# Remainder matmuls of a first MLP product run two at a time in halves of the array, at the head of groups of four column blocks

## The chip, the cores and the metric

One core of one Trainium2 chip. The metric is the device time of one execution in microseconds; the median of several executions is given, and the profile is that of one execution. "Ratio" always means the mean time of one kernel's fast runs over the mean of the other's fast runs in the same rounds on the same chip, so it is not quite the ratio of the medians that stand beside it. Brackets after a ratio are its 95% interval.

## The reference

Two layers, each an attention block and an MLP block, over 2048 tokens of width D = 576:

```python
x = x + attention(layernorm(x))      # 32 heads of 18, causal window of 256, softmax
y = layernorm(x)                     # no scale, no bias
h = gelu(y @ w1 + b1)                # w1: 576 x 4608
x = x + h @ w2 + b2                  # w2: 4608 x 576
```

What matters here is 576 = 4 x 128 + 64. A matmul contracts over at most 128 rows, so `y @ w1` takes four full steps and a remainder of 64 rows.

## The kernel before

The kernel is a list of tasks for five engines. A planner in the Python code places the tasks in time by estimated costs, chooses PSUM banks (the accumulators in which matmul results are collected, eight here), and so fixes the order of the instructions of each engine; the engines then run that order, each waiting on semaphores. A changed cost constant therefore changes nothing but the order.

Tokens go through in 8 chunks of 512 columns (four of each layer). In a chunk, `G_part` makes one half of the first MLP product: 18 column blocks of 128, each accumulated in one bank over five matmuls of 512 columns, and a gelu on ScalarE. `mm2` then makes the second product, with 288-column matmuls. Attention scores (`scores`) are matmuls with 32 rows; four of them run side by side in four strips of the array. [...] marks cuts.

```python
    B_O = 7                # bank of the attention output
    FILL = (6, 5, 4)       # banks of mm2, QKV, output projection
    MM1 = (0, 1, 2, 3)     # banks of the first MLP product
    SC = (0, 2, 4)         # bank pairs of the scores

    def mm_cost(n):        # the planner's cost of a matmul of n columns, us
        return max(n / 2400.0, 0.026) + (0.006 if n > 64 else 0.0)

    [...]  # start: rows 64 to 127 of the fifth chunk of w1, wqkv, wo and the columns 576 to 639 of xn are set to zero once
        add("dve", lambda e: e.memset(w1_sb[64:128, :, 2048:2560], 0.0), writes=["w1Z"], cost=1.0, prio=-8)

    [...]  # G_part: a tile w1_sb[:, sl] holds four column blocks
        for f in range(hf * NFH, (hf + 1) * NFH):
            sl = (k * 9 + f // 4) % NB1
            fl = f - hf * NFH
            bk = Bank(MM1)

            def fn(e, f=f, sl=sl, bk=bk):
                ins = None
                for c in range(KD):
                    col = c * 512 + (f % 4) * 128
                    ins = e.matmul(bank(bk)[:, 0:n], w1_sb[:, sl, col:col + 128], xnTm[:, k % 2, c, 0:n], start=(c == 0), stop=(c == KD - 1))
                return ins
            add("pe", fn, reads=[f"w1a{sl}", f"w1b{sl}_0", "w1Z"] + TXm, writes=[bk], cost=mm_cost(n) * 5, prio=prio, lat=0.15, alloc=[bk], fifo="pa",
                after=[f"h{fl}"])
            add("act", lambda e, f=f, fl=fl, bk=bk: e.activation(hT[:, fl, 0:n], bank(bk)[:, 0:n], ACT.Gelu_apprx_tanh,
                                                                bias=b1col[:, f:f + 1]),
                reads=[bk, "b1"], writes=[f"h{fl}"], cost=0.2 + n * 0.00087, lat=0.2, fifo="act", prio=prio)
            if f % 4 == 3:
                w1_load(prio - 2)

    [...]  # scores: four 32-row strips
                for j in range(4):
                    ins = e.matmul(two(bs[j // 2])[:, j % 2, col:col + nq * 128], kT[32 * j:32 * j + 32, g, (T0 + so) % KS, :],
                                   qT[32 * j:32 * j + 32, g, qo * 128:(qo + nq) * 128], start=True, stop=True, tile_position=(32 * j, 0))
```

The fifth matmul of a block (`c = 4`) has 64 rows of data and 64 rows of zeros. It costs as much as a full one: all 90 matmuls of a half stage step by the same 216 ns (next section).

The softmax here doesn't subtract the row's maximum and nothing guards it: scores larger than these inputs give would overflow.

## Time and profile before

| | before |
|---|---|
| median of 3 runs (lowest to highest) | 987.5 us (986.23 to 987.52) |
| span of the profiled execution | 987.9 us |
| PE, ScalarE, VectorE, GpSimd busy | 96%, 59%, 32%, 37% |
| first MLP product begins | 120.1 us |

PE is the matrix engine and PEld its weight loads; ACT is ScalarE, DVE VectorE, POOL GpSimd, SP the engine that issues most DMAs. The span is the time from the first instruction of the profiled execution to the last.

The page first: its part 1 (busy time and share of the span, by engine) and part 4 (the chain of work that ended last, by engine and by line). Line 751 is the first MLP product, 776 the second, 558 and 564 QKV and output projection, 628 the scores, 675 the attention output.

```profile
PE 949.5 (96%) x9592; PEld 606.9 (61%) x9592; DVE 317.1 (32%) x772; ACT 586.0 (59%) x705; POOL 368.8 (37%) x507
...
PE 78%; DMA 5%; DVE 5%; POOL 5%; ACT 4%; issue 3%; DVEq 0%; POOLq 0%
PE ps L776 29%; PE ps L751 27%; PE ps L558 7%; PE ps L675 7%; PE ps L628 6%; ACT pT L637 3%; POOL pT L658 2%; DMA attT<-attq 2%; DVE x_res L709 2%; PE ps L564 2%; POOL rstd L499 2%; DVE st_all L486 2%; DMA x_res<-in_A_x_dram 1%; DMA kT<-qn 
```

Three quarters of the chain is PE. PE is what the kernel waits for, and the first MLP product is 27% of the span.

Then groups of instructions of before, one line for each shape: line, engine, operation, output and inputs, shapes, count; busy time and mean duration of one; idle time of the engine before them and what ended it.

```profile
L751 PE MATMUL ps<-xnTm,w_sb 128*128 128x512 bf16 x1440 | 319.4, 379 | 0.1
L776 PE MATMUL ps<-w_sb,hT 128*128 128x288 bf16 x2304 | 316.1, 288 | 6.0 <-DVE x_res L709 4.9 <-DVE xn L712 1.1
...
L755 ACT ACTIVATE hT<-ps,b1col 128x512 bf16<-128x512 f32 x288 | 196.5, 687 | 251.1 <-PE ps L751 250.8
...
L628 PE MATMUL ps<-qT,kT 32*128 32x256 bf16 x448 | 24.3, 280 | 6.7 <-ACT pT L637 6.5
```

PE sat idle 0.1 us in all before the 1440 matmuls of the first product: they are on the critical path. The mean duration, 379 ns, is no cost, because matmuls overlap in the pipeline. The cost is the step from one start to the next, and it is read from the timeline of PE (start, duration of the merged row, line, count). One half stage of before:

```profile
910.32 19.59 PE L751 MATMUL ps<-xnTm,w_sb 128*128 128x512 bf16 x90
929.75 3.47 PE L776 MATMUL ps<-w_sb,hT 128*128 128x288 bf16 x27
```

Ninety matmuls from 910.32 to 929.75 us are 216 ns each, so a block costs five times that, 1.08 us. The same view in a stretch with scores:

```profile
384.65 1.63 PE L776 MATMUL ps<-w_sb,hT 128*128 128x288 bf16 x12
386.22 0.40 PE L628 MATMUL ps<-qT,kT 32*128 32x256 bf16 x8
386.55 0.91 PE L776 MATMUL ps<-w_sb,hT 128*128 128x288 bf16 x6
```

Twelve matmuls of 288 columns step by 122 ns, so the last starts at 384.65 + 11 x 0.122 = 385.99 us, and the first score follows 0.23 us later, not 0.122. Over the whole trace the median of that step is 218 ns, and it is 312 ns behind a 512-column matmul: 96 ns more than without a change of mode, either time. (The mode is the way the array is divided: whole, in halves or in strips.) On the way out, the step is 200 ns behind scores of 256 columns, where the next set of scores otherwise follows after 110, and 264 behind 384 columns, where it follows after 163. Behind 128 columns it is 147; the 53 ns at which the prediction puts these columns are an estimate (94 ns for the 224 columns between 288 and 512 give 54 for 128). So the way out costs some 90 to 101 ns more than the columns.

The waits of PE in before (who waited for whom: us in total, times, longest) are few and short:

```profile
PE ps L628 <- ACT pT L637: 8.4, 18, 1.4
PE ps L558 <- DVE qn L594: 5.0, 5, 1.0
PE ps L776 <- DVE x_res L709: 4.9, 10, 0.6
...
PE ps L675 <- ACT hT L755: 0.5, 3, 0.2
```

### The profile page before, as it was taken

What the parts mean: (1) busy time and instruction counts of PE and PEld (TensorE: products, weight loads), DVE (VectorE), ACT (ScalarE), POOL (GpSimd) and SP (SyncE); (2) the same over time, 40 slices, a digit from 0 to 9 for tenths busy, and PEclk for the clock granted to TensorE, in tenths of its full rate; (3) what the DMA queues carried; (4) which work ended last, traced back from release to release, by engine and by line L of the source; (5) the groups of instructions that cost most, each with busy time, mean ns of one, the idle gap of its engine ahead of it and who ended that gap; (6) DMA issues with size and microseconds to landing.
All of it is one profiled execution on the core that took longest, in us unless ns stands there. A gap on an engine that the chain in (4) does not pass through costs nothing.

```text
span 987.9 us, 22924 instructions
## 1 busy us (share of the span) xinstructions
PE 949.5 (96%) x9592; PEld 606.9 (61%) x9592; DVE 317.1 (32%) x772; ACT 586.0 (59%) x705; POOL 368.8 (37%) x507
## 2 busy tenths in 40 slices
PE   8898889999999999999999999999999999999998
PEld 6665547655575656756476565756567564657556
DVE  5653612722145211534028130361115310132001
ACT  0476676377753777447761777627774487852531
POOL 4555725334333434325153252433333352531000
PEclk9999899999999999999999999999999999999999
DMA  9846380964269250881529542494516816084540
GB/s 195 173 116 136 74 253 15 208 174 138 68 145 192 60 178 28 188 187 34 191 56 204 136 126 80 133 170 106 169 49 167 177 44 198 14 220 118 172 132 25
DMA packets 227287, 129.58 MB, mean 131 GB/s; under 512 B 141808, under 2 KB 225008, under 8 KB 227184
## 3 DMA queue, kind: packets, MB, share of 16 engines
q1 hardware_dynamic: 217872, 120.43, 49.4%
q0 software_dynamic: 6880, 5.03, 2.7%
q10 hardware_dynamic: 2432, 2.65, 0.9%
q8 instruction: 76, 1.25, 0.5%
q14 instruction: 27, 0.22, 0.1%
HBM read 90.69 MB, written 2.36 MB: 94 GB/s over the span
## 4 chain that ended last, share of the span: by engine, by line
PE 78%; DMA 5%; DVE 5%; POOL 5%; ACT 4%; issue 3%; DVEq 0%; POOLq 0%
PE ps L776 29%; PE ps L751 27%; PE ps L558 7%; PE ps L675 7%; PE ps L628 6%; ACT pT L637 3%; POOL pT L658 2%; DMA attT<-attq 2%; DVE x_res L709 2%; PE ps L564 2%; POOL rstd L499 2%; DVE st_all L486 2%; DMA x_res<-in_A_x_dram 1%; DMA kT<-qn 1%; DVE xn L509 1%
## 5 line engine op out<-in xcount | busy, mean ns | idle before, releaser
L637 ACT ACTIVATE pT<-ps 128x1024 bf16<-128x1024 f32 (+2 forms) x384 | 347.2, 971 | 128.1 <-PE ps L628 126.9
L658 POOL TENSOR_SCALAR_AFFINE_SELECT pT<-pT 128x512 bf16<-128x512 bf16 (+1 forms) x368 | 278.1, 778 | 388.2 <-ACT pT L637 365.4
L755 ACT ACTIVATE hT<-ps,b1col 128x512 bf16<-128x512 f32 x288 | 196.5, 687 | 251.1 <-PE ps L751 250.8
L776 PE MATMUL ps<-w_sb,hT 128*128 128x288 bf16 x2304 | 316.1, 288 | 6.0 <-DVE x_res L709 4.9
L751 PE MATMUL ps<-xnTm,w_sb 128*128 128x512 bf16 x1440 | 319.4, 379 | 0.1
L776 PEld LDWEIGHTS ps<-w_sb,hT 128*128 128x128 bf16 x2304 | 211.2, 98 | 80.6 <-issue 20.2
L751 PEld LDWEIGHTS ps<-xnTm,w_sb 128*128 128x128 bf16 x1440 | 139.5, 98 | 159.6 <-issue 0.4
L709 DVE TENSOR_TENSOR x_res<-ps,x_res 128x288 f32<-128x288 f32 x160 | 70.7, 449 | 363.4 <-PE ps L776 342.6
L558 PE MATMUL ps<-wqkv,xnTa 128*128 128x288 bf16 x768 | 120.5, 286 | 8.9 <-DVE qn L594 5.0
L675 PEld LDWEIGHTS ps<-vA,pT 128*128 128x128 bf16 x2880 | 94.2, 96 | 29.2 <-issue 11.7
L675 PE MATMUL ps<-vA,pT 128*128 128x20 bf16 x2880 | 100.6, 172 | 5.6 <-DVE attq L690 2.7
L558 PEld LDWEIGHTS ps<-wqkv,xnTa 128*128 128x128 bf16 x768 | 71.2, 97 | 33.1 <-DVE qn L594 7.8
L628 PE MATMUL ps<-qT,kT 32*128 32x384 bf16 (+2 forms) x1408 | 75.0, 280 | 11.6 <-ACT pT L637 8.4
L594 DVE CAST qn<-ps 128x288 bf16<-128x288 f32 x128 | 57.4, 455 | 39.2 <-PE ps L564 38.3
L486 DVE BATCH_NORM_STATS2 st_all<-x_res 128x6 f32<-128x288 f32 x120 | 50.8, 446 | 17.2 <-DMA x_res<-in_A_x_dram 15.9
L509 DVE TENSOR_SCALAR xn<-x_res,mv_all,rstd 128x576 bf16<-128x576 f32 x60 | 47.2, 801 | 26.1 <-POOL rstd L499 14.6
L564 PE MATMUL ps<-wqkv,xnTa 128*128 128x288 bf16 x192 | 54.9, 286 | 0.0
L628 PEld LDWEIGHTS ps<-qT,kT 32*128 32x128 bf16 x1408 | 22.4, 92 | 49.0 <-issue 24.7
L733 POOL TENSOR_TENSOR x_res<-x_res,b2bc 128x576 f32<-128x576 f32 x32 | 45.2, 1415 | 13.7 <-DVE xn L509 12.9
L712 DVE TENSOR_TENSOR xn<-ps,x_res 128x288 bf16<-128x288 f32 x32 | 14.6, 458 | 110.9 <-PE ps L776 110.9
L497 POOL TENSOR_SCALAR vtmp<-mv_all 128x1 f32<-128x1 f32 (+1 forms) x43 | 8.6, 200 | 103.9 <-DVE mv_all L488 101.4
L685 DVE RECIPROCAL rinv<-ps 128x16 f32<-128x16 f32 x64 | 16.4, 257 | 95.7 <-PE ps L675 95.4
(32 smaller groups left out, 332.7 us busy)
## 6 DMA issues: line engine op xcount, KB each, us to landing
w_sb<-in_B_w_dram SPq DMA_DIRECT2D x144, 288.0 KB, 5.1
w_sb<-in_B_w_dram SPq DMA_DIRECT2D x72, 512.0 KB, 4.0
w_sb<-in_B_w_dram SPq DMA_DIRECT2D x72, 64.0 KB, 3.7
x_res<-in_A_x_dram POOLq DMA_DIRECT2D x4, 1152.0 KB, 7.0
out_dram<-xn SPq DMA_DIRECT2D x16, 144.0 KB, 1.8
wqkv<-in_A_wqkv_dram ACTq DMA_DIRECT2D x3, 576.0 KB, 5.9
hT<-in_A_x_dram SPq DMA_DIRECT2D x1, 576.0 KB, 5.2
wo_sb<-in_A_wo_dram ACTq DMA_DIRECT2D x1, 576.0 KB, 4.0
```

Of the source, the lines that this page charges most:

```text
L486: add("dve", lambda e, i=i, s=s: e.bn_stats(st_all[:, t, i, :], s[:, t, i * HB:(i + 1) * HB]), reads=res, writes=[f"st{t}_{i}"], cost=0.43 ...
L558: ins = e.matmul(bank(bs[o])[:, 0:n], lhs(o, c, full), rhs(o, c, full), start=(c == 0), stop=False)
L564: ins = e.matmul(bank(bs[o])[:, 0:n], lhs(o, 4, full), rhs(o, 4, full), start=False, stop=True)
L594: add("dve", lambda e, o=o, b=bs[o], qv=qv: e.tensor_copy(qv[:, o * 16:(o + 1) * 16, 0:DH], bank(b)[:, 0:HB].rearrange("p (h d) -> p h d", ...
L628: ins = e.matmul(two(bs[j // 2])[:, j % 2, col:col + nq * 128], kT[32 * j:32 * j + 32, g, (T0 + so) % KS, :], qT[32 * j:32 * j + 32, g, qo ...
L637: add("act", lambda e, h2=h2: e.activation(pT[:, sl, 2 * h2:2 * h2 + 2, lo:hi], two(bs[h2])[:, :, lo:hi], ACT.Exp, scale=SCALE), reads=[bs ...
L658: add("pool", lambda e, ap=ap, pat=pat, sgn=sgn, kind=kind: e.affine_select(ap, ap, pattern=pat, compare_op=(ALU.is_ge if kind == "d" else ...
L675: ins = e.matmul(bank(B_O)[:, o:o + VW], pT[:, sl, j, col + qi * 128:col + (qi + 1) * 128], vA[:, (T0 + so) % VS, 4 * g + j, :], start=(fi ...
L709: add("dve", lambda e: e.tensor_tensor(x_res[:, t, sl], bank(b)[:, 0:HB], x_res[:, t, sl], ALU.add), reads=[b], writes=[f"x{t}h{hh}"], cos ...
L751: ins = e.matmul(bank(bk)[:, 0:n], w1_sb[:, sl, col:col + 128], xnTm[:, k % 2, c, 0:n], start=(c == 0), stop=(c == KD - 1))
L755: add("act", lambda e, f=f, fl=fl, bk=bk: e.activation(hT[:, fl, 0:n], bank(bk)[:, 0:n], ACT.Gelu_apprx_tanh, bias=b1col[:, f:f + 1]), rea ...
L776: ins = e.matmul(bank(b)[:, 0:HB], hT[:, fl, i * 128:(i + 1) * 128], w2_sb[:, fl, hh * HB:(hh + 1) * HB], start=(fl == 0), stop=(fl == NFH ...
```

## The change

The intent is to run two 64-row remainders at once, one in the lower and one in the upper half of the array, into two banks. Because changing between full and half mode costs time, the remainders of four blocks are run together at the head of a group, which needs four banks at once, and so the product may use all seven banks. The 18 blocks of a half stage give groups of 4, 4, 4, 4, 2 or 2, 4, 4, 4, 4. To feed the upper half, the remainder of w1 is loaded in two parts, and an extra VectorE instruction writes the last 64 normalised columns a second time. The planner's constant goes from 0.006 to 0.003 us. The rest of the diff removes an unused option (`PAIR`). Cut to its core:

```diff
-    MM1 = (0, 1, 2, 3)
+    MM1 = (0, 1, 2, 3, 4, 5, 6)
-        return max(n / 2400.0, 0.026) + (0.006 if n > 64 else 0.0)
+        return max(n / 2400.0, 0.026) + (0.003 if n > 64 else 0.0)
[...]
-            dma("sp", w1_sb[0:64, sl, 2048:2560], B_w1[512:576, cols], reads=["w1Z"], writes=[f"w1b{sl}_0"], ...)
+        src = B_w1[512:576, cols].rearrange("p (a b f) -> p b a f", a=2, b=2)
+        for b in range(2):
+            dma("sp", w1_sb[64 * b:64 * b + 64, sl, 2048:2304].rearrange("p (a f) -> p a f", a=2), src[:, b], ...)
[...]
-        for f in range(hf * NFH, (hf + 1) * NFH):          # one block: five full matmuls
+        while f < f1:
+            n4 = min(4 - f % 4, f1 - f)
+            fs = range(f, f + n4)
+            bks = [Bank(MM1) for _ in fs]
+            def rest(e, fs=fs, sl=sl, bks=bks):
+                for ff, bk in zip(fs, bks):
+                    b = ff % 2
+                    col = 2048 + (ff % 4) // 2 * 128
+                    ins = e.matmul(bank(bk)[:, 0:n], w1_sb[64 * b:64 * b + 64, sl, col:col + 128], xnTm[64 * b:64 * b + 64, k % 2, 4, 0:n],
+                                   start=True, stop=False, tile_position=(64 * b, 0))
+            add("pe", rest, reads=rd, writes=bks, cost=mm_cost(n) * (n4 // 2) + 0.21, alloc=bks, fifo="pa", ...)
+            for ff, bk in zip(fs, bks):                     # then four full matmuls a block, and its gelu
+                [...]
```

More of the change, by code (lines that the diff above doesn't have):

```diff
@@ L331, in schedule @@
         return max(t.end for t in self.tasks)
-PAIR = False
-W1W = 2560
 WARM_UNTIL = 140.0
@@ L373, in build_kernel @@
     x_res = sb("x_res", [P, NT, D], FP32)
-    w1_sb = sb("w1_sb", [P, NB1, W1W], BF16)
+    w1_sb = sb("w1_sb", [P, NB1, 2304], BF16)
     w2_sb = sb("w2_sb", [P, NFH, D], BF16)
@@ L449, in build_kernel @@
     add("pool", lambda e: e.memset(nhalf[:, :], -0.5), writes=["nhalf"], cost=0.1, prio=-10)
-    if not PAIR:
-        add("pool", lambda e: e.memset(xn[:, :, D:KD * 128], 0.0), writes=[f"xn{i}" for i in range(NXN)], cost=0.4, prio=-10)
+    add("pool", lambda e: e.memset(xn[:, :, D:KD * 128], 0.0), writes=[f"xn{i}" for i in range(NXN)], cost=0.4, prio=-10)
     add("pool", lambda e: e.memset(vA[:, :, :, DH:VW], 1.0), writes=[f"v{s}h{h}" for s in range(VS) for h in range(2)], cost=1.6, prio=-8)
@@ L455, in build_kernel @@
             writes=[f"qn{i}h{h}" for h in range(2)], cost=0.5, prio=-9)
-    if not PAIR:
-        add("pool", lambda e: e.memset(attq[:, :, D:KD * 128], 0.0), writes=["aqd"], cost=0.5, prio=-8)
-        add("dve", lambda e: e.memset(wqkv[64:128, 4, :], 0.0), writes=["wqC", "wkC", "wvC"], cost=1.0, prio=-8)
-        add("dve", lambda e: e.memset(wo_sb[64:128, 4, :], 0.0), writes=["woC"], cost=0.4, prio=-8)
-        add("dve", lambda e: e.memset(w1_sb[64:128, :, 2048:2560], 0.0), writes=["w1Z"], cost=1.0, prio=-8)
+    add("pool", lambda e: e.memset(attq[:, :, D:KD * 128], 0.0), writes=["aqd"], cost=0.5, prio=-8)
+    add("dve", lambda e: e.memset(wqkv[64:128, 4, :], 0.0), writes=["wqC", "wkC", "wvC"], cost=1.0, prio=-8)
+    add("dve", lambda e: e.memset(wo_sb[64:128, 4, :], 0.0), writes=["woC"], cost=0.4, prio=-8)
     dma("pool", b2bc[:, :], bass.AP(tensor=B_b2.tensor, offset=B_b2.offset, ap=[[0, P], [1, D]]), writes=["b2"], cls="b", ring=2,
@@ L502, in build_kernel, with ln_norm_T @@
     xn_ctr = [0]
-    def ln_norm_T(t, i, dst, dname, prio, src=None, srcres=None):
+    def ln_norm_T(t, i, dst, dname, prio, src=None, srcres=None, dup=False):
         s = x_res if src is None else src
@@ L512, in ln_norm_T @@
         rd = [f"xn{sl}"]
-        if PAIR:
+        if dup:
             add("dve", lambda e: e.tensor_scalar(xn[:, sl, D:KD * 128], s[:, t, 512:D], mv_all[:, t, 0:1], rstd[:, t:t + 1],
@@ L533, in w1_load @@
             reads=reads, writes=[f"w1a{sl}"], cls="w1", cost=0.5, prio=prio)
-        if PAIR:
-            src = B_w1[512:576, cols].rearrange("p (a b f) -> p b a f", a=2, b=2)
-            for b in range(2):
-                dma("sp", w1_sb[64 * b:64 * b + 64, sl, 2048:2304].rearrange("p (a f) -> p a f", a=2), src[:, b],
-                    writes=[f"w1b{sl}_{b}"], cls="w1", cost=0.5, prio=prio)
-        else:
-            dma("sp", w1_sb[0:64, sl, 2048:2560], B_w1[512:576, cols], reads=["w1Z"], writes=[f"w1b{sl}_0"], cls="w1", cost=0.5,
-                prio=prio)
+        src = B_w1[512:576, cols].rearrange("p (a b f) -> p b a f", a=2, b=2)
+        for b in range(2):
+            dma("sp", w1_sb[64 * b:64 * b + 64, sl, 2048:2304].rearrange("p (a f) -> p a f", a=2), src[:, b],
+                writes=[f"w1b{sl}_{b}"], cls="w1", cost=0.5, prio=prio)
     def w2_load(hf, prio, gate=False):
@@ L547, in w2_load, with two_out @@
                 reads=[f"h{2 * pr}"] if gate else [], writes=[f"w2s{pr}"], cls="w2", ring=9, cost=0.6, prio=prio)
-    def two_out(lhs, rhs, n, reads, prio, after=()):
+    def two_out(lhs, rhs, reads, prio, after=()):
         bs = [Bank(FILL), Bank(FILL)]
-        full = slice(0, 128)
         for o in range(2):
@@ L556, in fn @@
                 ins = None
-                for c in range(4):
-                    ins = e.matmul(bank(bs[o])[:, 0:n], lhs(o, c, full), rhs(o, c, full), start=(c == 0), stop=False)
-                if PAIR and o == 1:
-                    for oo in range(2):
-                        r = slice(64 * oo, 64 * oo + 64)
-                        ins = e.matmul(bank(bs[oo])[:, 0:n], lhs(oo, 4, r), rhs(oo, 4, r), start=False, stop=True, tile_position=(64 * oo, 0))
-                if not PAIR:
-                    ins = e.matmul(bank(bs[o])[:, 0:n], lhs(o, 4, full), rhs(o, 4, full), start=False, stop=True)
-                return ins
-            w = [bs[0], bs[1]] if (o == 1 and PAIR) else [bs[o]]
-            cost = mm_cost(n) * (4 if PAIR else 5) + (mm_cost(n) * 1.2 if PAIR and o == 1 else 0.0)
-            add("pe", fn, reads=reads, writes=w, cost=cost, prio=prio, alloc=((bs if o == 0 else ()) if PAIR else [bs[o]]), after=after)
+                for c in range(KD):
+                    ins = e.matmul(bank(bs[o])[:, 0:HB], lhs(c), rhs(c, o * HB), start=(c == 0), stop=(c == KD - 1))
+                return ins
+            add("pe", fn, reads=reads, writes=[bs[o]], cost=mm_cost(HB) * KD, prio=prio, alloc=[bs[o]], after=after)
         return bs
@@ L579, in qkv @@
             dest = [f"v{A % VS}h{o}" for o in range(2)] if w == "v" else [f"qn{qn_ctr[0] % NQN}h{o}" for o in range(2)]
-            bs = two_out(lambda o, c, r: xnTa[r, c, i * 128:(i + 1) * 128],
-                         lambda o, c, r, n=n: wqkv[r, c, n * D + o * HB:n * D + (o + 1) * HB], HB,
+            bs = two_out(lambda c: xnTa[:, c, i * 128:(i + 1) * 128], lambda c, s, n=n: wqkv[:, c, n * D + s:n * D + s + HB],
                          [f"w{w}A", f"w{w}B", f"w{w}C", f"xa{i}"], prio + 0.01 * n, after=dest)
@@ L717, in tail @@
         rd = [f"aq{g}" for g in range(G)]
-        if PAIR:
-            add("dve", lambda e: e.tensor_copy(attq[:, 0:nt, D:KD * 128], attq[:, 0:nt, 512:D]), reads=rd, writes=["aqd"], cost=0.25,
-                prio=prio)
         for i in range(nt):
@@ L725, in tail @@
             t = t0 + i
-            bs = two_out(lambda o, c, r, i=i: attT[r, c, i * 128:(i + 1) * 128],
-                         lambda o, c, r: wo_sb[r, c, o * HB:(o + 1) * HB], HB, [f"aT{i}", "woA", "woB", "woC"], prio)
+            bs = two_out(lambda c, i=i: attT[:, c, i * 128:(i + 1) * 128], lambda c, s: wo_sb[:, c, s:s + HB],
+                         [f"aT{i}", "woA", "woB", "woC"], prio)
             for o in range(2):
@@ L731, in tail @@
             ln_rstd([t], True, prio)
-            ln_norm_T(t, i, xnTm[:, k % 2], f"xm{k % 2}_", prio)
+            ln_norm_T(t, i, xnTm[:, k % 2], f"xm{k % 2}_", prio, dup=True)
             add("pool", lambda e, t=t: e.tensor_tensor(x_res[:, t, :], x_res[:, t, :], b2bc[:, :], ALU.add),
@@ L741, in G_part @@
         TXm = [f"xm{k % 2}_{i}" for i in range(nt)]
-        for f in range(hf * NFH, (hf + 1) * NFH):
-            sl = (k * 9 + f // 4) % NB1
-            fl = f - hf * NFH
-            bk = Bank(MM1)
-            def fn(e, f=f, sl=sl, bk=bk):
-                ins = None
-                for c in range(KD):
-                    col = c * 512 + (f % 4) * 128
-                    ins = e.matmul(bank(bk)[:, 0:n], w1_sb[:, sl, col:col + 128], xnTm[:, k % 2, c, 0:n], start=(c == 0), stop=(c == KD - 1))
-                return ins
-            add("pe", fn, reads=[f"w1a{sl}", f"w1b{sl}_0", "w1Z"] + TXm, writes=[bk], cost=mm_cost(n) * 5, prio=prio, lat=0.15, alloc=[bk], fifo="pa",
-                after=[f"h{fl}"])
-            add("act", lambda e, f=f, fl=fl, bk=bk: e.activation(hT[:, fl, 0:n], bank(bk)[:, 0:n], ACT.Gelu_apprx_tanh,
-                                                                bias=b1col[:, f:f + 1]),
-                reads=[bk, "b1"], writes=[f"h{fl}"], cost=0.2 + n * 0.00087, lat=0.2, fifo="act", prio=prio)
-            if f % 4 == 3:
+        f1 = (hf + 1) * NFH
@@ new lines, in G_part, with fn @@
+        f = hf * NFH
+        while f < f1:
+            n4 = min(4 - f % 4, f1 - f)
+            fs = range(f, f + n4)
+            f += n4
+            sl = (k * 9 + fs[0] // 4) % NB1
+            bks = [Bank(MM1) for _ in fs]
+            rd = [f"w1a{sl}", f"w1b{sl}_0", f"w1b{sl}_1"] + TXm
+            def rest(e, fs=fs, sl=sl, bks=bks):
+                ins = None
+                for ff, bk in zip(fs, bks):
[3 more added lines that the diff above has]
+                                   start=True, stop=False, tile_position=(64 * b, 0))
+                return ins
+            add("pe", rest, reads=rd, writes=bks, cost=mm_cost(n) * (n4 // 2) + 0.21, prio=prio, alloc=bks, fifo="pa",
+                after=[f"h{ff - hf * NFH}" for ff in fs])
+            for ff, bk in zip(fs, bks):
+                fl = ff - hf * NFH
+                def fn(e, ff=ff, sl=sl, bk=bk):
+                    ins = None
+                    for c in range(4):
+                        col = c * 512 + (ff % 4) * 128
+                        ins = e.matmul(bank(bk)[:, 0:n], w1_sb[:, sl, col:col + 128], xnTm[:, k % 2, c, 0:n], start=False, stop=(c == 3))
+                    return ins
+                add("pe", fn, reads=rd, writes=[bk], cost=mm_cost(n) * 4, prio=prio, lat=0.15, fifo="pa")
+                add("act", lambda e, ff=ff, fl=fl, bk=bk: e.activation(hT[:, fl, 0:n], bank(bk)[:, 0:n], ACT.Gelu_apprx_tanh,
+                                                                      bias=b1col[:, ff:ff + 1]),
+                    reads=[bk, "b1"], writes=[f"h{fl}"], cost=0.2 + n * 0.00087, lat=0.2, fifo="act", prio=prio)
+            if fs[-1] % 4 == 3:
```

## The prediction

> **What bounds the kernel now.** TensorE. The page gives PE 96% busy; the chain of waits puts 78% of the span on PE (29% second MLP matmul, 27% first). Busy time overstates pipelined matmuls, so I count start to start: in PE's timeline a 512-column matmul of the first MLP product takes 216 ns, a 288-column one 122, a 20-column one 25. Such steps sum to about 793 of the 848 us after 140 us; about 30 us of the rest is switching to and from the 32-row score matmuls, some 25 us waits. The other engines have slack (ScalarE 59%).
>
> **What the change does.** Today each of 288 column blocks runs 5 matmuls of 512 columns, the fifth half zeros. Afterwards 4 full ones; the 64-row remainders run as 144 pairs, in 80 groups (64 of four blocks, 16 of two, because 18 blocks per half don't divide by four).
> - Removed: 288 x 0.216 = 62.2 us.
> - Added: 144 pairs. The Trainium skill (TensorE: Matmul & The Clock Gate, Part 3) says matmuls in different row groups run together, about 4 ns apart; the trace agrees: scores in four 32-row strips start 3 ns apart, and the next set follows 163 ns after 384 columns. So 0.219 us a pair: 31.5 us.
> - Added: 80 mode switches in and out. The skill (TensorEngine Tiling, Key Properties) says changing mode drains the array, without a figure. The trace shows it at the scores: from a full 512-column matmul to the first score 312 ns instead of 216 (96 extra); out of the scores 147 where 128 columns need 53 (94 extra). So 0.19 us a group: 15.2 us, an estimate carried over from 32-row to 64-row strips.
>
> Net on PE: 62.2 - 31.5 - 15.2 = 15.5 us. A group of two gains only 0.02.
>
> **Critical path.** Nearly all first-MLP matmuls lie on it: PE waits 0.1 us before them (groups).
>
> Given back: a group needs four banks at once, keeps the later ones about 3 us longer, and takes banks that the second MLP matmul, QKV and scores use too. Over 16 half stages I allow 1 to 3 us of new waits, where a group, or the first scores after it, waits for gelus. The extra VectorE copy of 64 columns and 72 more DMA issues on the SP queue are off the path. The finer cost constant reorders the plan; either sign, a few us.
>
> **Prediction: 973.5 us (-1.4%), 8 in 10 within 966 to 982. Faster by over 2%: 0.13; within 2%: 0.84; slower by over 2%: 0.03.**
>
> **What would show each step right or wrong.**
> - Groups: 1152 full 512-column matmuls and 288 with 64 rows; in the timeline the two of a pair start 3 ns apart, pairs 216 ns apart. If they serialise, the time rises by up to 31 us.
> - The step from a full matmul into a remainder about 312 ns, and out of it about 310. If switching costs 0.4 us a group, the gain is gone; if nothing, it is about 30 us.
> - Waits: PE on ScalarE before remainders or scores, under 5 us more than now.
> - A closed group of four takes about 4.1 us of PE, against 4.32.
>
> **What would make it wrong.** A 64-row switch that costs differently; a second pair whose weights cannot load behind the first; bank starvation where second-MLP matmuls and groups share seven banks; a plan that runs PE dry where exponentials limit.

## The result, and the profile after

| | before | after |
|---|---|---|
| median of 6 runs | 987.51 us (986.23 to 989.44) | 972.62 us (969.24 to 973.67) |
| ratio | | 0.9841 [0.982, 0.9861] |
| span of the profiled execution | 987.9 us | 967.4 us |
| PE busy | 96% | 96% |

The profiled execution of the changed kernel was the fastest of its six (969.24 us), so its trace shows 20.5 us of difference where the medians show 14.9. In later calls the same kernel gave 0.9822 and 0.9806. It is about 15 to 20 us faster, some 1.8%.

The same two parts of the page after. Line 748 is now the full matmuls of the first product, 736 its remainders, 772 the second product, 548 QKV and output projection, 609 the scores, 656 the attention output.

```profile
PE 933.4 (96%) x9596; PEld 582.3 (60%) x9596; DVE 324.6 (34%) x803; ACT 588.0 (61%) x705; POOL 370.5 (38%) x507
...
PE 82%; DMA 6%; POOL 4%; DVE 3%; issue 2%; ACT 2%; SPq 0%; POOLq 0%; DVEq 0%
PE ps L772 29%; PE ps L748 24%; PE ps L548 12%; PE ps L656 7%; PE ps L609 6%; PE ps L736 4%; POOL pT L639 2%; ACT pT L618 2%; DMA attT<-attq 2%; DVE x_res L690 1%; DMA xnTa<-xn 1%; DVE st_all L481 1%; DMA x_res<-in_A_x_dram 1%; DMA kT<-qn 1
```

The groups of the changed kernel; 509 is the added VectorE copy:

```profile
L772 PE MATMUL ps<-w_sb,hT 128*128 128x288 bf16 x2304 | 316.8, 288 | 5.6 <-DVE x_res L690 3.6 <-ACT hT L751 1.0 <-DVE xn L693 0.8
...
L748 PE MATMUL ps<-xnTm,w_sb 128*128 128x512 bf16 x1152 | 266.3, 380 | 0.0
...
L751 ACT ACTIVATE hT<-ps,b1col 128x512 bf16<-128x512 f32 x288 | 197.9, 688 | 215.7 <-PE ps L748 215.1
...
L736 PE MATMUL ps<-xnTm,w_sb 64*128 64x512 bf16 x288 | 45.0, 382 | 0.9 <-ACT pT L618 0.9
...
L509 DVE TENSOR_SCALAR xn<-x_res,mv_all,rstd 128x64 bf16<-128x64 f32 x32 | 10.9, 340 | 0.0
```

There are 1152 full matmuls and 288 with 64 rows, as intended. Gelu takes what it took (197.9 against 196.5 us).

A half stage of the changed kernel in the timeline of PE, to be held against the 90 matmuls in one row before:

```profile
927.81 0.39 PE L736 MATMUL ps<-xnTm,w_sb 64*128 64x512 bf16 x2
928.13 1.90 PE L748 MATMUL ps<-xnTm,w_sb 128*128 128x512 bf16 x8
929.96 0.61 PE L736 MATMUL ps<-xnTm,w_sb 64*128 64x512 bf16 x4
930.50 3.63 PE L748 MATMUL ps<-xnTm,w_sb 128*128 128x512 bf16 x16
934.06 0.60 PE L736 MATMUL ps<-xnTm,w_sb 64*128 64x512 bf16 x4
934.60 3.63 PE L748 MATMUL ps<-xnTm,w_sb 128*128 128x512 bf16 x16
```

From one head to the next, 929.96 to 934.06, a group of four takes 4.10 us; before it took 20 x 0.216 = 4.32. A group of two (927.81 to 929.96) takes 2.15 us against 2.16 before. The four remainders and the switch out take 0.54 us (929.96 to 930.50); the switch in lies in the step before. Inside, the two of a pair start 3 to 4 ns apart, and the second pair follows 222 to 224 ns after the first in 62 of the 64 groups of four. The median step from a full 512-column matmul into a remainder is 312 ns, and from a remainder to a full one 308.5.

The waits of PE after, none of which grew to anything:

```profile
PE ps L609 <- ACT pT L618: 4.3, 10, 1.3
PE ps L656 <- POOL pT L639: 3.8, 7, 1.4
PE ps L772 <- DVE x_res L690: 3.6, 6, 1.2
...
PE ps L736 <- ACT pT L618: 0.9, 2, 0.7
```

The first MLP product waited for banks 0.9 us in all.

I summed the steps between the starts of successive matmuls, from the first matmul of the first MLP product to the end, in the trace of each kernel. A step's nominal part is its columns' time (216 ns for 512 columns, 122 for 288, 25 for 20). A switch of mode is counted as 0.095 us each way, so the switches of the table are a count of switches times that price, and no measured sum. What lies above is a wait, or, in stretches where the records give half the TensorE clock, clock loss. In some traces 3 to 5% of the records of the full matmuls are missing; their time was put back from the known counts. All in us; all of these are single profiled executions:

| kernel | first MLP product starts | its matmuls, full + remainder | switches for it | waits | clock loss | span |
|---|---|---|---|---|---|---|
| before | 120.1 | 310.8 | 0 | 25.5 | 2.5 | 987.9 |
| after | 121.4 | 248.6 + 31.8 | 15.1 | 19.5 | 2.4 | 967.4 |
| after_again (first call) | 120.8 | 248.6 + 31.8 | 15.1 | 21.9 | 2.8 | 969.2 |
| after_third (third call) | 121.7 | 248.6 + 31.8 | 15.1 | 18.8 | 1.4 | 965.7 |
| before_new_cost | 119.5 | 310.8 | 0 | 18.4 | 1.5 | 978.6 |
| group_full | 121.7 | 310.8 | 0 | 21.8 | 4.0 | 985.8 |
| group_full_old_cost | 122.1 | 310.8 | 0 | 25.1 | 3.3 | 989.6 |
| half_serial | 121.8 | 248.6 + 62.1 | 15.1 | 25.1 | 4.9 | 1006.3 |
| groups_of_two | 117.4 | 248.6 + 31.2 | 27.3 | 21.9 | 1.6 | 979.7 |
| after_old_cost | 120.0 | 248.6 + 32.2 | 15.1 | 21.8 | 1.5 | 968.2 |
| banks_0_3 | 119.8 | 248.6 + 35.3 | 15.1 | 50.8 | 12.2 | 1006.4 |
| groups_6444 | 119.8 | 248.6 + 34.4 | 12.1 | 51.2 | 11.5 | 1003.8 |
| qkv_pairs | 126.4 | 248.6 + 32.0 | 26.9 (QKV's included) | 22.2 | 3.0 | 980.2 |
| halves_throughout | 118.7 | 284.5 | 8.8 | 50.0 | 13.5 | 998.6 |

The remaining PE work (second MLP product, QKV, output projection, attention) is 494.7 us of steps before and 493.2 after, and 29.4 us of switching for the scores in both: the same, but for qkv_pairs, whose QKV takes 8.1 us less, and groups_of_two, where some 2 us more of it falls behind the start of the first MLP product.

### The profile page after: what moved, and what is told of

Same layout as the page of the kernel before. It is cut to its first block, busy times and chain, and to the rows that moved or that the text cites. A ratio compares the mean times of both kernels' runs of the same rounds, so it can differ in the third digit from the quotient of the medians.

```text
span 967.4 us, 23096 instructions
## 1 busy us (share of the span) xinstructions
PE 933.4 (96%) x9596; PEld 582.3 (60%) x9596; DVE 324.6 (34%) x803; ACT 588.0 (61%) x705; POOL 370.5 (38%) x507
## 4 chain that ended last, share of the span: by engine, by line
PE 82%; DMA 6%; POOL 4%; DVE 3%; issue 2%; ACT 2%; SPq 0%; POOLq 0%; DVEq 0%
PE ps L772 29%; PE ps L748 24%; PE ps L548 12%; PE ps L656 7%; PE ps L609 6%; PE ps L736 4%; POOL pT L639 2%; ACT pT L618 2%; DMA attT<-attq 2%; DVE x_res L690 1%; DMA xnTa<-xn 1%; DVE st_all L481 1%; DMA x_res<-in_A_x_dram 1%; DMA kT<-qn 1%; DMA xnTm<-xn 1%
## 5 line engine op out<-in xcount | busy, mean ns | idle before, releaser
L751 ACT ACTIVATE hT<-ps,b1col 128x512 bf16<-128x512 f32 x288 | 197.9, 688 | 215.7 <-PE ps L748 215.1
L748 PE MATMUL ps<-xnTm,w_sb 128*128 128x512 bf16 x1152 | 266.3, 380 | 0.0
L748 PEld LDWEIGHTS ps<-xnTm,w_sb 128*128 128x128 bf16 x1152 | 105.8, 98 | 141.1 <-issue 28.6
L548 PE MATMUL ps<-wqkv,xnTa 128*128 128x288 bf16 x960 | 129.9, 287 | 5.1 <-DMA xnTa<-xn 2.1
L656 PEld LDWEIGHTS ps<-vA,pT 128*128 128x128 bf16 x2880 | 95.4, 96 | 26.9 <-issue 8.0
L548 PEld LDWEIGHTS ps<-wqkv,xnTa 128*128 128x128 bf16 x960 | 89.1, 98 | 34.4 <-issue 4.7
L504 DVE TENSOR_SCALAR xn<-x_res,mv_all,rstd 128x576 bf16<-128x576 f32 x60 | 44.8, 754 | 43.2 <-DMA xnTm<-xn 26.2
L711 POOL TENSOR_TENSOR x_res<-x_res,b2bc 128x576 f32<-128x576 f32 x32 | 45.7, 1429 | 26.9 <-DVE xn L509 23.6
L548 PE MATMUL ps<-wo_sb,attT 128*128 128x288 bf16 x320 | 43.2, 286 | 4.3 <-DMA attT<-attq 3.1
L736 PE MATMUL ps<-xnTm,w_sb 64*128 64x512 bf16 x288 | 45.0, 382 | 0.9 <-ACT pT L618 0.9
```

What stands on the lines that cost most here:

```text
L548: ins = e.matmul(bank(bs[o])[:, 0:HB], lhs(c), rhs(c, o * HB), start=(c == 0), stop=(c == KD - 1))
L656: ins = e.matmul(bank(B_O)[:, o:o + VW], pT[:, sl, j, col + qi * 128:col + (qi + 1) * 128], vA[:, (T0 + so) % VS, 4 * g + j, :], start=(fi ...
L736: ins = e.matmul(bank(bk)[:, 0:n], w1_sb[64 * b:64 * b + 64, sl, col:col + 128], xnTm[64 * b:64 * b + 64, k % 2, 4, 0:n], start=True, stop ...
L751: add("act", lambda e, ff=ff, fl=fl, bk=bk: e.activation(hT[:, fl, 0:n], bank(bk)[:, 0:n], ACT.Gelu_apprx_tanh, bias=b1col[:, ff:ff + 1]), ...
```

## The experiments

The theory to be tested: the gain is 31 us of array time saved by running remainders in pairs, less some 15 us of switching; the regrouping, the banks and the new order of the plan are small. The rivals: the order of the plan (the constant) brought the gain; pairs are only recorded side by side and save nothing; switching is nearly free and the rest was lost to banks. Kernels of one call ran on one chip, with their own runs of before. after_again, group_full, half_serial and groups_of_two were one call (before 988.06 us); before_new_cost, after_old_cost, banks_0_3 and groups_6444 another (986.51); group_full_old_cost, after_third, qkv_pairs and halves_throughout a third (986.98). The planner plans each version anew, so each comparison also holds a change of the order, which by itself was worth up to 6 us (before_new_cost, group_full_old_cost).

### after_again: the changed kernel in the first call

Unedited.

> The changed kernel itself, unedited, so that the other kernels of this call have it beside them on the same chip. Every theory: about 972.6 us, within 969 to 974; ratio to before 0.984.

Measured: 970.70 us, ratio 0.9822 [0.9805, 0.9838]. As expected.

### group_full: groups, banks and plan without pairs

The w1 layout and zeros of before, no second copy of columns, and:

```diff
-  e.matmul(bank(bk)[:, 0:n], w1_sb[64 * b:64 * b + 64, sl, col:col + 128], xnTm[64 * b:64 * b + 64, k % 2, 4, 0:n],
-           start=True, stop=False, tile_position=(64 * b, 0))
+  e.matmul(bank(bk)[:, 0:n], w1_sb[:, sl, col:col + 128], xnTm[:, k % 2, 4, 0:n], start=True, stop=False)
-  cost=mm_cost(n) * (n4 // 2) + 0.21
+  cost=mm_cost(n) * n4
```

> Groups, seven banks and the new cost constant kept; the remainders run at the head of the group, but as full 128-row matmuls with zeros, as before. No halves, no switch of mode. Theory (the gain is 31.1 us of pairing minus 15.2 us of switching, the rest is neutral): the gain disappears, 986 to 990 us. Rival 1 (the order of the plan, the groups and the three more banks brought the gain): 970 to 976 us. Rival 2 (pairing and switching as I say, but the grouping costs some 5 us that the plan hides): 991 to 995 us.

Measured: 986.18 us, ratio 0.9981 [0.9968, 0.9994]. The gain is gone. What pairing adds to this kernel is 986.18 - 970.70 = 15.5 us. Rival 1 fails as far as it concerns the regrouped kernel. Rival 2 fails in its number, but a cost of the grouping that the plan hides does come out below (group_full_old_cost).

### half_serial: both switches, but nothing side by side

The w1 layout of before, no second copy of columns, and every remainder in the lower half:

```diff
-  w1_sb[64 * b:64 * b + 64, sl, col:col + 128], xnTm[64 * b:64 * b + 64, k % 2, 4, 0:n], ..., tile_position=(64 * b, 0))
+  w1_sb[0:64, sl, col:col + 128], xnTm[0:64, k % 2, 4, 0:n], ..., tile_position=(0, 0))
-  cost=mm_cost(n) * (n4 // 2) + 0.21
+  cost=mm_cost(n) * n4 + 0.21
```

> As the changed kernel, with the mode switches, but all remainders lie in the lower half of the array, so the two of a pair cannot run together. Theory: 144 times 0.216 us more than the changed kernel, plus 31 us, so about 1003 us (1000 to 1006), and steps of 216 ns between the four remainders in place of 4, 216, 4. Rival (the halves don't really save time, the two of a pair are only recorded side by side): no more than 5 us over the changed kernel.

Measured: 1007.94 us, ratio 1.0213 [1.0188, 1.0238], 37 us over the changed kernel and above the expected range. The timeline of PE (734 are the remainders, 746 the full matmuls):

```profile
967.13 1.03 PE L734 MATMUL ps<-xnTm,w_sb 64*128 64x512 bf16 x4
968.10 3.63 PE L746 MATMUL ps<-xnTm,w_sb 128*128 128x512 bf16 x16
971.66 0.60 PE L734 MATMUL ps<-xnTm,w_sb 64*128 64x512 bf16 x2
```

A group takes 4.53 us (967.13 to 971.66), 0.43 more than in the changed kernel: two more matmuls of 0.216. The table has 30.3 us more of remainders. The other 6 us, which I had not expected, are waits (3.2 us more than in after_again), clock loss (2.1 more) and a start 1.0 us later. So the pairs do run together, and that is worth some 30 us.

### groups_of_two: more switches

```diff
-            n4 = min(4 - f % 4, f1 - f)
+            n4 = 2
```

> Pairs kept, but every group has two blocks: 144 switches of mode in place of 80. Theory (a switch in and out costs 0.19 us whatever follows): 64 times 0.19 = 12.2 us more than the changed kernel, about 985 us (982 to 988). Rival (switching is nearly free, and what the change gave back was lost because a group holds four banks): groups of two hold fewer banks, so the time stays or falls, 968 to 973 us.

Measured: 980.12 us, ratio 0.9918 [0.9903, 0.9933], 9.4 us over the changed kernel. The timeline:

```profile
943.55 0.39 PE L736 MATMUL ps<-xnTm,w_sb 64*128 64x512 bf16 x2
943.88 1.90 PE L748 MATMUL ps<-xnTm,w_sb 128*128 128x512 bf16 x8
945.71 0.39 PE L736 MATMUL ps<-xnTm,w_sb 64*128 64x512 bf16 x2
```

Two blocks take 2.16 us (943.55 to 945.71), just what they took before the change: one switch in and out eats one saved matmul of 512 columns. The 27.3 us of switching against 15.1 in the table is the expected 12.2 by count. By the medians of the traces it is 13.0: a head takes 0.538 us with four remainders and 0.322 with two, and the step into it 0.096 more. The time rose by less, 9.4, below the expected range. In this order of the plan the first MLP product began at 117.4 us, 3.4 us earlier than in after_again, though some 2 us of QKV and attention matmuls moved behind that point, and clock loss was 1.2 us less; single traces show no more of the cause. The rival (fewer banks held, so as fast or faster) fails.

### before_new_cost: the plan's constant alone

```diff
-        return max(n / 2400.0, 0.026) + (0.006 if n > 64 else 0.0)
+        return max(n / 2400.0, 0.026) + (0.003 if n > 64 else 0.0)
```

> The kernel before with one number of the change: the plan's constant per matmul 0.003 in place of 0.006 us, which only reorders the instructions. Theory (pairing and switching make the gain, the plan some 2 us of it, as the run with full remainders in groups showed): 984 to 989 us. Rival (the finer constant brought most of the gain): 970 to 978 us.

Measured: 981.37 us, ratio 0.9938 [0.9922, 0.9955]. Both theories missed: the constant alone makes the old kernel 5 us faster, as much as a third of the whole gain. In the trace it is mostly waits, 18.4 against 25.5 us, in the same work.

### after_old_cost: the changed kernel without the new constant

The reverse edit in the changed kernel.

> The changed kernel with the old constant, 0.006 us. Theory: within 4 us of the changed kernel (967 to 975 us), the streaming and switching times of its trace unchanged, only waits moved. Rival (the finer constant is what keeps PE from waiting): above 976 us.

Measured: 970.71 us, ratio 0.9845 [0.9826, 0.9864]. Against 0.9806, 0.9822 and 0.9841 for the changed kernel, the constant is worth between nothing and 0.4% here. The whole change does not need it.

### group_full_old_cost: regrouping alone

group_full with the constant 0.006.

> Grouping and seven banks alone, with full zero-padded remainders and with the old plan constant: neither pairs nor the finer constant. If grouping costs some 4 us by itself (the difference of the two runs with the new constant): 989 to 993 us. If those 4 us were only one order of the plan against another: 984 to 988 us, as before within 2 us.

Measured: 990.36 us, ratio 1.0041 [1.0024, 1.0059]. With this the parts can be laid side by side, each as the ratio to before in its own call (each known to about 0.2% either way):

| | old constant | new constant |
|---|---|---|
| kernel before | 1 | 0.9938 |
| regrouped, seven banks, full remainders | 1.0041 | 0.9981 |
| regrouped, seven banks, pairs | 0.9845 | 0.9841, 0.9822, 0.9806 |

Regrouping by itself costs 0.4% (4 us) under either constant, the new constant gives back 0.6% (6 us), and pairing gives 1.6% under the new constant (0.9981 less the mean of the three, 0.9823), which is the 15.5 us, and 2.0% under the old one. The old column's excess over 15.5 us goes with waits: 25.1 us in group_full_old_cost, 21.8 in after_old_cost.

### banks_0_3: the groups with the four banks of before

```diff
-    MM1 = (0, 1, 2, 3, 4, 5, 6)
+    MM1 = (0, 1, 2, 3)
```

> The changed kernel, but the groups may use banks 0 to 3 only, as before, in place of 0 to 6. Theory (the three more banks are what keeps the grouping from costing anything): the next group cannot start until the last gelu of this one has read its bank, about 1 us after PE's last matmul, where no other matmul fills in; for perhaps half of the 80 groups that is 40 us, so 990 to 1025 us, with PE waits on the gelu line before the remainders. Rival (banks don't matter, other work fills every hole): within 4 us of the changed kernel.

Measured: 1007.64 us, ratio 1.0211 [1.0195, 1.0228]. The timeline of all engines shows the expected wait (751 is the gelu):

```profile
968.54 3.63 PE L748 MATMUL ps<-xnTm,w_sb 128*128 128x512 bf16 x16
...
971.35 0.69 ACT L751 ACTIVATE hT<-ps,b1col 128x512 bf16<-128x512 f32 x1 [0.18 <-PE ps L748]
972.21 0.69 ACT L751 ACTIVATE hT<-ps,b1col 128x512 bf16<-128x512 f32 x1 [0.18 <-PE ps L748]
...
973.04 0.61 PE L736 MATMUL ps<-xnTm,w_sb 64*128 64x512 bf16 x4 [0.87 <-ACT hT L751]
...
973.58 3.63 PE L748 MATMUL ps<-xnTm,w_sb 128*128 128x512 bf16 x16
```

The sixteen full matmuls end, the gelu of the last block runs from 972.21 to 972.90 us, and only then can the next head start, at 973.04, after 0.87 us in which PE had nothing to do. A group takes 5.04 us (968.54 to 973.58), more than before the change. Against the traces of the changed kernel, waits are 29 to 32 us more, and the loss to the lower clock 9 to 11 us more. But this wait is the smaller part of it. Of the waits of PE in this run:

```profile
PE ps L548 <- DMA attT<-attq: 16.3, 7, 3.5
...
PE ps L736 <- ACT hT L751: 7.1, 10, 0.9
```

Remainders waited 7.1 us for gelus, 10 times; the largest sum is output projections that waited 16.3 us for the transposed attention output, against 3.1 us in the changed kernel. The expected sum (half of the 80 groups, 40 us) came out about right by another road: how four banks leave PE without other work at those places, by the order of the plan or otherwise, is not shown.

### groups_6444: fewer switches, more banks at once

The loop goes over groups of 6, 4, 4 and 4 blocks, across the tiles of w1 (each block takes its own tile; the rest as in the change):

```diff
-            n4 = min(4 - f % 4, f1 - f)
-            fs = range(f, f + n4)
+        for n4 in (6, 4, 4, 4):
+            fs = range(f, f + n4)
```

> The changed kernel with the 18 blocks of a half in four groups of 6, 4, 4 and 4 (across the weight tiles) in place of five: 64 switches in place of 80. If switching alone counted, 16 times 0.19 = 3.0 us less than the changed kernel, 965 to 969 us. Rival, which I hold the likelier: a group of six takes six of the seven banks at once, and PE waits for banks more than the 3.0 us that it saves, 975 to 995 us; the trace then shows 12.2 us of switching in place of 15.2 and more waits.

Measured: 1005.51 us, ratio 1.0196 [1.0177, 1.0214]. The rival that I held likelier was right in kind, and low in size. Switching fell to 12.1 us as computed, and waits rose by some 30 us, the largest of them (12.8 us) before QKV matmuls, on the VectorE copies that free such banks:

```profile
PE ps L548 <- DVE qn L575: 12.8, 11, 2.8
```

The other products may hold three banks of `FILL` at a time; seven less three is four. So four is the largest group that leaves them their banks; that this is the reason is argued from the wait above, not tested apart.

### after_third: the changed kernel in the third call

> The changed kernel again, unedited, so that the kernels of this call have it beside them on the same chip: 968 to 974 us, ratio 0.982 to 0.986.

Measured: 966.54 us, ratio 0.9806 [0.978, 0.9831]: below what was expected, though the interval overlaps those of the other calls. What differs from call to call is not settled; the same order of instructions ran each time.

### qkv_pairs: the same trick on a smaller matmul

QKV makes two 288-column outputs for each 128 tokens, with the same 64-row remainder. Both halves of the fifth weight chunk are loaded, the normalised columns are written twice, and one pair opens each double output:

```diff
+                if o == 0:
+                    for oo in range(2):
+                        r = slice(64 * oo, 64 * oo + 64)
+                        ins = e.matmul(bank(bs[oo])[:, 0:HB], lhs(r, 4), rhs(r, 4, oo * HB), start=True, stop=False, tile_position=(64 * oo, 0))
-                for c in range(KD):
+                for c in range(4):
```

> The changed kernel, and the 64-row remainders of QKV run in pairs too: one pair of 288 columns for each of 96 double outputs, each with its own switch of mode. Theory (a switch costs 0.19 us whatever the columns; a lone pair of 288 columns saves 0.122 us): 96 times (0.19 + 0.003 - 0.122) = 6.8 us more than the changed kernel, about 978 us (974 to 982), with 18.2 us more of switching in the trace. Rival (what counts is the number of matmul steps on PE, switching hides behind other work): 11.7 us less than the changed kernel, 957 to 962 us.

Measured: 982.74 us, ratio 0.9953 [0.9933, 0.9973], 16.2 us over the changed kernel of the call. The direction was right and the size low. After the first MLP product begins, the trace has 11.8 us more switching and 8.1 us less streaming (66 outputs at 0.122), a loss of 3.7 where the same rates over all 96 give 6.8. In the rest, the first MLP product begins 4.7 us later, of which the 30 pairs that run before it make up to 3.1 at these rates, and waits and clock loss are 5.0 us higher; the new order, the second copy of all columns and the additional weight loads were not told apart. The timeline (563 the pair, 565 the eight full matmuls of QKV):

```profile
640.00 0.81 PE L765 MATMUL ps<-xnTm,w_sb 128*128 128x512 bf16 x3
640.74 0.30 PE L563 MATMUL ps<-wqkv,xnTa 64*128 64x288 bf16 x2
640.97 1.15 PE L565 MATMUL ps<-wqkv,xnTa 128*128 128x288 bf16 x8
```

The last of the three 512-column matmuls starts at 640.43, so the pair starts 0.31 us later, and the first full matmul 0.23 us after the pair, where 288 columns need 0.12: again 0.1 us for each change of mode.

### halves_throughout: no switch inside a group at all

All first-MLP matmuls are 64-row, one block of a pair in the lower half and the other in the upper half, with its own bank:

```diff
+                for c in range(9):
+                    for o in range(2):
+                        r = slice(64 * o, 64 * o + 64)
+                        ins = e.matmul(bank(bks[o])[:, 0:n], w1_sb[r, sl, col:col + 128], xnTm[r, k % 2, c, 0:n],
+                                       start=(c == 0), stop=(c == 8), tile_position=(64 * o, 0))
```

For this all normalised columns are written twice (one VectorE instruction of 1.47 us), w1 comes in 256-byte pieces, and to make room three rings (sets of buffers used in turn) were cut (qn 6 to 4, xn 4 to 2, v 10 to 8). The doubled columns have a buffer of their own, `xnd`, and only one.

> All first-MLP matmuls in halves of the array: a block of each pair has its 9 chunks of 64 rows in the lower half, the other in the upper half, so mode is switched only where a stretch of first-MLP matmuls begins or ends, and a step takes two banks, not four. It needs the normalised rows twice, weights in 256-byte pieces, and some smaller buffers to make room. Theory (switching is paid per entry and exit): about 95 one-way switches in place of 159, 9 us in place of 15.1, so about 6 us less than the changed kernel, 961 to 968 us, if the smaller buffers and smaller DMA pieces cost nothing. Rival (the smaller pieces or buffers starve PE, or the two halves don't load weights fast enough): over 975 us, with PE waiting on weight DMA or with steps longer than 216 ns.

Measured: 997.48 us, ratio 1.0106 [1.0085, 1.0128]. Both theories were half right. Switching fell to 8.8 us, and 1296 pairs streamed in 284.5 us, 0.2195 each, so two halves do load weights fast enough. But PE waited 50.0 us. The waits of PE:

```profile
PE ps L656 <- POOL pT L639: 10.9, 10, 6.7
PE ps L609 <- ACT pT L618: 7.4, 15, 1.6
PE ps L609 <- DVE x_res L690: 6.8, 3, 5.0
PE ps L548 <- DVE qn L575: 6.5, 7, 2.9
PE ps L766 <- DMA w_sb<-in_B_w_dram: 5.3, 1, 5.3
```

They are spread over attention, QKV and the second product's weights. Which of the smaller rings, the longer VectorE instruction and the smaller DMA pieces caused them was not separated by a run. The trace of the longest wait points to the single buffer `xnd`:

```profile
219.03 1.47 DVE L711 TENSOR_SCALAR xnd<-x_res,mv_all,rstd 128x1152 bf16<-128x1152 f32 x1 [6.51 <-DMA xnTm<-xnd]
220.58 1.40 POOL L717 TENSOR_TENSOR x_res<-x_res,b2bc 128x576 f32<-128x576 f32 x1 [6.57 <-DVE xnd L711]
...
223.68 0.60 PE L656 MATMUL ps<-vA,pT 128*128 128x20 bf16 x16 [6.68 <-POOL pT L639]
```

VectorE waited 6.5 us until a transpose had read `xnd`, GpSimd waited for VectorE, and PE for the masks that GpSimd wrote next. In all VectorE waited 76.7 us for `xnd` here; where the changed kernel normalises, it waited 26.2 us for such transposes. No version tried beats the changed kernel.

## Why the prediction was right

The prediction was 973.5 us and the first result 972.62, within 2% of before, as it gave 84%. The later calls of the same kernel (970.70 and 966.54 us) lie 3 and 7 us below it, still in its range.

- *Removed and added matmuls: 62.2 less 31.5 = 30.7 us.* Right. The trace has 310.8 before and 280.4 after, 30.4 less; half_serial, which undoes only the running side by side, has these 30 us back.
- *Two of a pair together.* Right, 3 to 4 ns apart, as in the 32-row strips. The second pair follows after 223 ns, not 216, a small miss.
- *0.19 us a group for switching, 15.2 us.* Right: the median step is 312 ns in and 308.5 out, where 512 columns take 216, so 0.19 us; and by the medians 64 more groups cost 13.0 us in groups_of_two, 0.20 each. (The 15.1 and 27.3 us of the table are counts times this price.) The figure taken from 32-row scores held for 64-row halves, and for another width in qkv_pairs.
- *Almost all of it on the critical path.* Right: group_full and the changed kernel differ by 15.5 us, the net of the PE arithmetic. That it agrees to the tenth is luck: by the intervals it is known to some 2 us, and under the old constant the same comparison gives 19 us.
- *1 to 3 us given back for banks.* A little low: regrouping alone costs 4 us (2.4 to 5.8 by the interval). The three added banks keep it that small: without them the changed kernel is 37 us slower (1007.64 against 970.71 us for after_old_cost).
- *The new constant, either sign, a few us.* In sign open, in size right: 5 to 6 us faster where regrouping stands alone or is absent, between nothing and 4 us with pairs. So two terms of opposite sign nearly cancelled, and the agreement within 1 us is partly luck. The arithmetic of 15.5 us is borne out by its parts, the steps in the timeline and half_serial.
- *Waits, under 5 us more.* Right. All waits together were 6 us fewer in the traced execution (19.5 against 25.5). The constant is at most a part of the reason, since after_old_cost has 21.8.
- A mistake in the text of the prediction: the steps were summed over the last 858.6 us of the span (from 129.3 us), not the last 848 (from 140). The trace's clock starts before the span. It changes none of the terms.

## What to carry to other kernels

A pair of half-height matmuls saves one matmul's columns and pays 0.19 us for going into half mode and back; here that means a lone pair of 512 columns breaks even, a lone pair of 288 loses, and two pairs of 512 behind one switch gain 0.22 us (4.32 less 4.10; 0.235 by the sum of the parts). Read the price of a switch from any place in the trace where the kernel already changes mode, and the count of switches from the loop; then ask how many banks a group may hold at once, because here two banks more for one group in each half stage made the kernel some 35 us slower, more than twice the price of all switches together. Where a planner fixes the order, run the regrouping without the trick, under the old and the new cost constant: a reordering of this size is worth several us by itself, and can hide or imitate a gain.

## What the Trainium skill lacked or had wrong

- "TensorEngine Tiling (Array Packing)", Key Properties, says that changing the tiling mode drains the array and gives no price. Here it is 96 ns on the way in (312 against 216 ns) and some 93 on the way out (308.5 against 216), much the same for 32-row strips (96 in, 90 to 101 out) as for 64-row halves. So one pair of 512 columns between full matmuls gained nothing (2.16 us for two blocks with it and without); the gain needs several pairs behind one switch.
- "TensorE: Matmul & The Clock Gate", Back-to-back issue gap, gives a sustained 131 ns for a matmul of 512 columns in a stream of weight loads and matmuls, and calls 216 ns the isolated gap. The 90 matmuls of the half stage before are such a stream, and take 216 ns each.
- The same page, Part 3, says in its list of what overlaps that a weight load overlaps running matmuls only when their row groups differ, while its paragraph on the mechanism also lets a load into the background weight buffer be pulled ahead. In half_serial all remainders lie in one row group, and their median step is 216 ns, the time of the columns: the weight load (94 ns) is hidden there too, so the list by itself is too narrow.
- The same page, HAM oscillation, gives "no PE-idle gaps >~3.4µs" as the rule for keeping the clock. In banks_0_3, waits of 2.5, 2.8 and 2.9 us (at 425, 657 and 776 us) were each followed within 5 us by 3.4 us at half clock, and clock loss there came to 12.2 us against 2.4. A wait of 2.4 us in the profiled run of the changed kernel was not, nor was the longest of banks_0_3 itself, 3.7 us at 307 us. So in these runs a wait may be shorter than the rule's and be followed by the low clock, or longer and not; its length alone did not decide, and what does is not settled here. The 3.4 us after those three waits agree with the page's window; other stretches of that run lasted 6.8 and 10.2 us.
